# Grouping a pair's transposes in one run of the tensor engine, and spreading value products between keys

## The chip, the cores and the metric

The kernel runs on one core of one Trainium2 chip. The metric is the device time of one execution in microseconds. The engines are PE (matrix products; PEld is its loading of weights), DVE (vector), ACT (scalar), POOL (GpSimd) and SP, which issues the transfers.

## The reference

Windowed attention with 32 global tokens, for 8 batches of 8 heads, and then a feed-forward layer on the result:

```python
s_g = scale * np.matmul(q_g, k_all.transpose(0, 1, 3, 2))
out_g = np.matmul(sm(s_g), v_all)
mask = np.abs(pos[:, None] - pos[None, :]) <= window        # window = 32
s_l = np.concatenate([s_lg, np.where(mask, s_ll, -1e9)], axis=-1)
out_l = np.matmul(sm(s_l), np.concatenate([v_g, v_l], axis=2))
x = np.concatenate([out_g, out_l], axis=2)                   # 8 x 544 tokens x (8 heads x 64)

x_prev = np.concatenate([zeros, x[:, :-1, :]], axis=1)
xk = mu_k * x + (1.0 - mu_k) * x_prev
xr = mu_r * x + (1.0 - mu_r) * x_prev
k = np.maximum(xk @ w_k, 0.0)                                # 512 -> 1024
v = k * k @ w_v                                              # 1024 -> 512
r = 1.0 / (1.0 + np.exp(-(xr @ w_r)))                        # 512 -> 512
out = r * v
```

Local sequences have 512 tokens, global ones 32, heads 64 columns.

## The kernel before

**Number format.** Each feed-forward operand is split into a high and a low part (`h`, `l`), and a product is made of three matmuls (high-high, high-low, low-high). The high part is a cast, the low part the rest: `Keys.part` does both for one half of an operand. The cast is always DVE's (L740), the rest (L741) is DVE's for operands whose name begins with B and POOL's for the others (T1 to T4).

**Two kinds of work.** Attention is done in pairs of units; a unit is two heads of one batch, so a batch has four units in two pairs. The feed-forward layer works on the two token halves of a batch, t0 and t1. While the feed-forward layer of batch b runs, the attention of batch b + 1 is computed, for b = 1 to 6. From batch 2 on, the value product is made for both halves at once by Strassen's scheme: seven products per batch with operands B11, B21, T2 (`values_1`), then T3, T1, T4, B22 (`values_2`). T1 to T4 are differences of the B operands (`Keys.difference`, L733, on DVE). Their left sides lie in DRAM and are loaded as tiles `a`, half a megabyte each, two per product.

**The order is written out by hand.** In this stage PE, ACT, DVE and POOL execute in the order in which the program writes; SP's order is found by a scheduler. `in_turn` goes through a string of letters (`BATCH`): A is the next step of the generator `attention`, F the next step of the batch's feed-forward work (`batch`). One F is 24 matmuls of 128x256. Behind the matmuls of F number n, the entries of the table `todo` for n are written (splits, differences, and `mixing`, which makes xk and xr), and then one entry of the queue `softmaxes` (exponentials of ACT, sums' inverses of DVE, products of POOL for the pair whose scores were last computed).

**A pair's attention before** has seven A steps: four times four transposes of the probabilities (`transposes`, L144; ACT copies each four into `PT`, L414), one step with half of the global transposes, one with the other half and the next pair's scores (128 small matmuls into four banks, reduced on DVE by sixteen instructions, L368), one with the next pair's global scores and this pair's value products (L141 with `PT`).

**Banks of PSUM.** Feed-forward products take the three `ps_m` banks in turn. The transposes take the single `ps_t` bank. The scores take the four `ps_s` banks, and so do, in the same rotation, the global scores (one bank) and the value products (three banks). So the global scores go to the bank in which the first four of the sixteen score blocks lay. A product with `fresh=False` (B22) adds to the bank of an earlier one (T1).

**Feed-forward steps of a batch before** are three products V1, four keys of t0, two gates, four products V2, four keys of t1, two gates.

Of the kernel before, what the change touches and what calls it, by code (L numbers as in the profile page):

```python
# [11 lines left out]
F32R = mybir.dt.float32r  # L12
# [54 lines left out]
def local_global_attention_then_rwkv_ffn(  # L67
# [12 lines left out]
    nc = tc.nc  # L80
# [39 lines left out]
    def psum(tag):  # L120
        if isinstance(use[tag], str):
            tag = use[tag]
        n = turn[tag] = turn.get(tag, -1) + 1
        pool = use[tag][n % len(use[tag])]
        return pool.tile([P, 512], F32, tag="ps", name=f"ps_{tag}")
# [173 lines left out]
        finish(*last)  # L299

    V1 = (("A11", "B11"), ("A12", "B21"), ("S2", "T2"))
    V2 = (("S3", "T3"), ("S1", "T1"), ("A22", "T4"), ("S4", "B22"))
    to_load = [a for a, _ in V1 + V2] * (B - FROM) + ["A11", "A21", "A12", "A22"]
    left = []

# [98 lines left out]
    def pitched(j, h, g0, n):  # L404
        return PT[:, j, h, g0 * PITCH:(g0 + n) * PITCH].rearrange("p (g q) -> p g q", g=n)[:, :, 0:W]

    def transposes(r, h, j=None):

        tp = psum("t")
        for i in range(4):  # L410
            last = transpose(tp[:, i * P:(i + 1) * P], r.Pt[:, 4 * h + i], ident)
        copy = nc.scalar.copy
        if j is not None:
            copy(pitched(j, h, 0, 4), tp.rearrange("p (g q) -> p g q", g=4))  # L414
        else:
            g0 = 2 * r.slots[0][1]
            out = PT[:, :, h, g0 * PITCH:(g0 + 2) * PITCH].rearrange("p j (g q) -> p j g q", g=2)[:, :, :, 0:W]
            copy(out, tp.rearrange("p (j g q) -> p j g q", j=2, g=2))
        return last
# [282 lines left out]
    class Keys:  # L702
# [42 lines left out]
            self.difference(b, i)  # L745
            self.part(b, i)

        def left_over(self, n):

            part, difference = self.part, self.difference  # L750
            todo = (
                ((part, "T2", 1), (difference, "T3", 1)),
                ((part, "T3", 0), (difference, "T4", 0)),
                ((part, "T3", 1), (part, "T1", 0), (difference, "T4", 1)),
                ((part, "T1", 1),),
                ((part, "T4", 0),),
                ((part, "T4", 1), (part, "B22", 0)),
                ((part, "B22", 1),),
            )
            for what, b, i in todo[n]:  # L760
                what(b, i)

        def split(self, *names):
            for b in names:
                self.parts[b] = []
                for val in self.k[b]:
                    tags = Keys.PARTS[Keys.n_parts % len(Keys.PARTS)]
                    Keys.n_parts += 1
                    h, l = (self.tokens[0].two(mlp, f"b{x}", F32R, tag) for x, tag in zip("hl", tags))
                    split(val, h, l, nc.vector if b[0] == "B" else nc.gpsimd)  # L770
                    self.parts[b].append((h, l))

        def product(self, out, b, fresh=True, apart=False, between=None):
            right = self.parts.pop(b)
            steps = [(i, j) for i in range(HC) for j in range(2)]
# [40 lines left out]

        def values_2(self):
            t0, t1 = self.tokens
            u2, u3, c22 = self.u2, self.sum(), self.sum()
            X = self.bank()  # L820
            self.product(X, "T3")
            nc.vector.tensor_add(u3, X, u2)
            yield
            Y = self.bank()
            self.product(Y, "T1")
            nc.vector.tensor_add(c22, Y, u3)
            t1.write(1, c22)
            yield
            X = self.bank()
            self.product(X, "T4")  # L830
            nc.vector.tensor_add(u3, X, u3)
            t0.write(1, u3)
            yield
            self.product(Y, "B22", fresh=False)
            nc.vector.tensor_add(u2, Y, u2)
            t1.write(0, u2)
            yield
# [38 lines left out]
    def attention(pairs):  # L876

        for s in pairs[0]:
            load_qk(s)
        for s in pairs[0]:  # L880
            load_v(s)
        yield
        R = [scores(whole(s)) for s in pairs[0]]
        yield
        Pg = scores_global(pairs[0])
        for pair, nxt in zip(pairs, pairs[1:] + [None]):
            xTs = [xT_of(s.b, s.c) for s in pair]
            for s in nxt or ():
                load_qk(s)
            for j, r in enumerate(R):  # L890
                for h in range(2):
                    transposes(r, h, j)
                    yield
            transposes_global(Pg, (0,))
            yield
            transposes_global(Pg, (1,))
            by_hand = line["all"]
            if nxt:
                R = [scores(whole(s), by_hand) for s in nxt]
                if by_hand:  # L900
                    exps, norm = ([f for r in R for f in of(r)] for of in (lambda r: r.exps, lambda r: r.norm))
                    exps[0]()
                    for i in range(3):
                        softmaxes.append((norm[i], exps[i + 1]))
            yield
            if not by_hand:
                yield
            if nxt:
                Pg, *softmax = scores_global(nxt, later=True)
            copied = weighted(pair, xTs, True)  # L910
            if nxt:
                if by_hand:
                    softmaxes.append((norm[3], softmax[0]))
                    softmaxes.append((softmax[1],))
                else:
                    with tc.issue_after(copied.ins):
                        for f in softmax:
                            f()
            for s in nxt or ():
                load_v(s)  # L920
            yield pair[1].c + 1 == NC
# [146 lines left out]
    def batch(b, before):  # L1068
# [33 lines left out]
        def begin_halves():  # L1102
            nonlocal leftp, sump, gate3
            early_u.close()
            leftp, sump, gate3 = (
                place(name, bufs) for name, bufs in (("leftp", 5), ("sump", 3), ("gate3", 1))
            )
            load_left()
            load_left()
# [22 lines left out]
                15: lambda: (mix_next("r0"), this.difference("T3", 0)),  # L1132
            }
        else:
            steps = chain(before.values_1(), this.keys(t0), gates_of(0), before.values_2(), this.keys(t1), gates_of(1))
            todo = {
                0: lambda: (before.left_over(0), mix(t0, "r2")),
                1: lambda: before.left_over(1),
                2: lambda: before.left_over(2),
                3: lambda: before.left_over(3),  # L1140
                4: lambda: before.left_over(4),
                6: lambda: mix(t1, "k0"),
                7: lambda: mix(t1, "k2"),
                8: lambda: mix(t1, "r0"),
                9: lambda: before.left_over(5),
                10: lambda: (before.left_over(6), mix(t1, "r2")),
                11: lambda: this.part("B11", 0),
                12: lambda: (this.part("B11", 1), this.part("B21", 0)),
                13: lambda: (this.part("B21", 1), this.difference("T1", 0)),
                14: lambda: this.difference("T1", 1),  # L1150
                15: lambda: this.made("T2", 0),
                16: lambda: (this.difference("T2", 1), mix_next("k0")),
                17: lambda: mix_next("k2"),
                18: lambda: (mix_next("r0"), this.difference("T3", 0)),
            }
        for n, _ in enumerate(steps):
# [10 lines left out]
    def keys_at(b):  # L1167
# [2 lines left out]
        return keys_of[b]  # L1170

    BATCH = {
        FROM - 1: "AFAFAFAFAF" "AFFAFFF" "AFAFAFAFAF" "AFFAFFF",
        FROM: "AFAFAFAFAF" "AFAF" "AFAFAFAFAF" "AFFAFF",
        None: "AFAFAFAFAF" "AFFAFF" "AFAFAFAFAF" "AFFFAFF",
    }
    last = first[1]
    change_use(MIDDLE_USE)
# [16 lines left out]
    def end():  # L1195
        change_use(LAST_USE)
        keys, gates = final.keys(t), t.gates()
        values, ends = chain(last.values_1(), last.values_2()), final.values_of_one()
        at, to = last.part, last.difference
        todo = (  # L1200
            lambda: (at("T2", 1), to("T4", 0)),
            lambda: (to("T4", 1), to("T3", 1), at("T3", 0)),
            lambda: (at("T3", 1), at("T1", 0)),
            lambda: (at("T1", 1), at("T4", 0)),
            lambda: t.mixing("r2"),
            lambda: (at("T4", 1), at("B22", 0)),
            lambda: None,
            lambda: at("B22", 1),
            lambda: final.part("B11", 0),
            lambda: (final.part("B11", 1), final.part("B21", 0)),  # L1210
            lambda: final.part("B21", 1),
        )
        for n, x in enumerate("VVKVKVKVKVVEGEGEE"):
            next({"K": keys, "V": values, "E": ends, "G": gates}[x], None)
            if n < len(todo):
                todo[n]()
            yield
# [51 lines left out]
```

## Time and profile before

| | |
|---|---|
| median of three runs | 657.32 us (654.34 to 665.51) |
| profiled execution | 657.44 us |
| its span | 655.7 us |
| busy share of the span: PE, DVE, POOL, ACT | 96%, 78%, 53%, 52% |
| transfers | 127 MB, 194 GB/s |
| clock of PE granted over the span | 0.995 |

In the profile, `L141` is the one line that records all matmuls, and `L144` the one for transposes, so groups are told apart by tile names: `ps_m` feed-forward, `ps_s` scores and value products, `ps_t` transposes. Consecutive matmuls overlap: one has a modelled duration of 0.28 us, but the next starts 0.12 us after it.

The batches lie in the span like this: 1 from 125 to 200 us, 2 to 267, 3 to 340, 4 to 411, 5 to 482, 6 to 550; batch 7, which has no attention beside it, to 604; then the global tokens to the end.

### The profile page before, as it was taken

To read this page: it belongs to the slowest core of one execution; us is meant where nothing else is said; L and a number is where in the kernel's file an instruction comes from. 1 tells how busy PE (TensorE), PEld (TensorE's weight loads), DVE (VectorE), ACT (ScalarE), POOL (GpSimd) and SP (SyncE) were. 2 spreads that over 40 slices of the span, in tenths; PEclk is the share of its full clock that TensorE was granted. 3 is DMA by queue.
4 is the path that set the end of the run, shared out by engine and by line. 5 is a ranking of instruction groups with operands and counts; after the bars stand their busy time and mean duration, and the time that the engine had idled before them with its cause. 6 is when DMAs were issued, how large, how long until landed. Compare 5 with 4: busy or idle time off the path is not lost.

```text
span 655.7 us, 20533 instructions
## 1 busy us (share of the span) xinstructions
PE 630.7 (96%) x8362; PEld 599.6 (91%) x8362; DVE 510.9 (78%) x1308; ACT 338.4 (52%) x1062; POOL 348.4 (53%) x318
## 2 busy tenths in 40 slices
PE   6789899999999989999999999999999999999998
PEld 3567889999989989989999999989999999999997
DVE  4699986556898677986989698986898687787980
ACT  4888686637263576464463727364745533314111
POOL 6377775334856242764357443855366535652840
PEclk9799999999999999999999999999999999999999
DMA  9826534538366922727555584737383562462774
GB/s 333 353 98 241 177 137 163 170 111 307 128 218 208 332 95 73 278 57 289 204 214 190 193 303 163 240 110 267 136 288 103 190 229 67 144 227 79 240 232 170
DMA packets 43565, 127.15 MB, mean 194 GB/s; under 512 B 4048, under 2 KB 20944, under 8 KB 43472
## 3 DMA queue, kind: packets, MB, share of 16 engines
q1 hardware_dynamic: 43472, 125.85, 54.6%
q8 instruction: 66, 1.08, 0.6%
q14 instruction: 27, 0.22, 0.1%
HBM read 108.53 MB, written 17.30 MB: 192 GB/s over the span
## 4 chain that ended last, share of the span: by engine, by line
PE 78%; DVE 10%; DMA 4%; ACT 3%; POOL 2%; issue 2%; SPq 1%; DVEq 0%; ACTq 0%; POOLq 0%
PE ps_m L141 60%; PE ps_s L141 12%; PE ps_t L144 4%; DMA w<-w_k 2%; DMA w<-w_v 1%; DVE diff L614 1%; DVE xfull L582 1%; PE ps_t L141 1%; POOL wv_l L240 1%; ACT Pt L374 1%; DVE a L272 1%; DVE ps_s L230 1%; DVE ps_s L227 1%; DVE kkl L641 1%; DVE bh L740 1%
## 5 line engine op out<-in xcount | busy, mean ns | idle before, releaser
L141 PE MATMUL ps_m<-xkh,wk_h 128*128 128x256 f32 x544 | 155.6, 286 | 2.7 <-DVE gate L685 0.9
L141 PE MATMUL ps_m<-xkl,wk_h 128*128 128x256 f32 x544 | 151.6, 279 | 1.2 <-POOL xkl L587 1.2
L141 PE MATMUL ps_m<-xkh,wk_l 128*128 128x256 f32 x544 | 150.9, 278 | 0.0
L141 PE MATMUL ps_m<-bh,a 128*128 128x256 f32 x736 | 137.3, 283 | 0.0
L380 POOL TENSOR_TENSOR Pt<-Pt,ssum 128x512 f32<-128x512 f32 x64 | 69.6, 1093 | 89.5 <-DVE ssum L333 45.5
L141 PEld LDWEIGHTS ps_m<-bh,a 128*128 128x128 f32 x736 | 115.0, 189 | 0.0
L141 PEld LDWEIGHTS ps_m<-xkh,wk_h 128*128 128x128 f32 x544 | 102.2, 188 | 8.5 <-issue 2.4
L374 ACT ACTIVATE Pt<-Pt,m 128x128 f32<-128x128 f32 x256 | 99.2, 390 | 16.8 <-DVE m L368 16.5
L141 PEld LDWEIGHTS ps_m<-xkl,wk_h 128*128 128x128 f32 x544 | 102.5, 188 | 2.1 <-POOL xkl L587 1.4
L141 PE MATMUL ps_m<-bl,a 128*128 128x256 f32 x368 | 103.0, 280 | 0.0
L141 PEld LDWEIGHTS ps_m<-xkh,wk_l 128*128 128x128 f32 x544 | 102.4, 188 | 0.0
L656 ACT ACTIVATE relu<-ps_m 128x512 f32<-128x512 f32 x52 | 31.0, 596 | 90.3 <-PE ps_m L141 89.8
L141 PE MATMUL ps_m<-xrh,wr_h 128*128 128x256 f32 x272 | 77.0, 283 | 0.0
L141 PE MATMUL ps_m<-xrl,wr_h 128*128 128x256 f32 x272 | 75.6, 278 | 0.0
L141 PE MATMUL ps_m<-xrh,wr_l 128*128 128x256 f32 x272 | 75.4, 278 | 0.0
L619 POOL TENSOR_TENSOR xkl<-xfull,xkh 128x512 fp32r<-128x512 f32 x30 | 39.7, 1325 | 66.5 <-DVE ssum L332 43.1
L141 PEld LDWEIGHTS ps_m<-bl,a 128*128 128x128 f32 x368 | 69.6, 189 | 0.0
L414 ACT COPY PT<-ps_t 128x512 f32<-128x512 f32 x56 | 32.8, 585 | 67.7 <-PE ps_t L144 67.7
L619 POOL TENSOR_TENSOR xrl<-diff,xrh 128x512 fp32r<-128x512 f32 x30 | 40.7, 1356 | 46.8 <-DVE xrh L618 29.8
L368 DVE CUSTOM_DVE_ANT_0 Pt<-ps_s,masks 128x128 f32<-128x128 f32 x256 | 55.9, 285 | 12.0 <-PE ps_s L141 12.0
L141 PE MATMUL ps_s<-raw_qk 64*32 64x128 f32 (+1 forms) x2112 | 55.4, 287 | 5.4 <-DMA raw_qk<-qk 5.4
L741 POOL TENSOR_TENSOR bl<-B,bh 128x512 fp32r<-128x512 f32 x36 | 51.9, 1459 | 14.3 <-DVE bh L740 13.9
(128 smaller groups left out, 1522.1 us busy)
## 6 DMA issues: line engine op xcount, KB each, us to landing
a<-scratch SPq DMA_DIRECT2D x92, 512.0 KB, 4.8
raw_v<-v SPq DMA_DIRECT2D x32, 896.0 KB, 7.6
raw_qk<-qk SPq DMA_DIRECT2D x32, 624.0 KB, 5.5
out_l<-gate SPq DMA_DIRECT2D x32, 256.0 KB, 4.1
w<-w_k SPq DMA_DIRECT2D x8, 512.0 KB, 9.4
w<-w_v SPq DMA_DIRECT2D x8, 512.0 KB, 4.1
w<-w_r SPq DMA_DIRECT2D x4, 512.0 KB, 3.2
scratch<-wv_h SPq DMA_DIRECT2D x8, 256.0 KB, 3.8
```

The costliest lines, as they stand in the source:

```text
L141: return in_line(nc.tensor.matmul(*a, **kw))
L144: return in_line(nc.tensor.transpose(*a, **kw))
L227: nc.vector.tensor_scalar(bits, word(I32, 1), 3, 0x7FFFFFF8, op0=ALU.logical_shift_left, op1=ALU.bitwise_and)
L230: nc.vector.scalar_tensor_tensor(bits, word(I32, 1), -(2 ** 31), bits, op0=ALU.bitwise_and, op1=ALU.bitwise_or)
L240: engine.tensor_sub(lo, val, hi.bitcast(F32))
L368: read = nc.vector.tensor_tensor_reduce(out=Pt[:, i], in0=place(t, n, h), in1=masks[:, 2 * slots[t][1] + n], op0=ALU.add, op1=ALU.min, sca ...
L374: nc.scalar.activation(Pt[:, i], Pt[:, i], AF.Exp, bias=low_x[:, i:i + 1], scale=-1.0, accum_out=ssum[:, i:i + 1],)
L380: nc.gpsimd.tensor_mul(Pt[:, some], Pt[:, some], inv.unsqueeze(2).to_broadcast([P, 4, W]))
L414: copy(pitched(j, h, 0, 4), tp.rearrange("p (g q) -> p g q", g=4))
L619: nc.gpsimd.tensor_sub(lo[:, both], xf, hi[:, both].bitcast(F32))
L656: nc.scalar.activation(rk, kp, AF.Relu)
L741: (nc.vector if b[0] == "B" else nc.gpsimd).tensor_sub(l, val, h.bitcast(F32))
```

## The change

Four things change in the stage that is ordered by hand. First, the sixteen transposes of a pair and the first half of the global ones form one A step, and the sixteen write the four `ps_s` banks instead of taking turns in `ps_t`; a pair has three A steps. Second, the F steps of a batch come in another order: keys stand between the value products. Third, T4's product comes before T1's, and its sum has a tile of its own (`sump` has four). Fourth, `todo` places the splits and differences elsewhere, and `BATCH` the A steps. The number of matmuls, splits and softmax instructions stays.

```diff
@@ V2
-    V2 = (("S3", "T3"), ("S1", "T1"), ("A22", "T4"), ("S4", "B22"))
+    V2 = (("S3", "T3"), ("A22", "T4"), ("S1", "T1"), ("S4", "B22"))
@@ transposes
-    def transposes(r, h, j=None):
+    def transposes(r, h, j=None, bank="t"):
 
-        tp = psum("t")
+        tp = psum(bank)
@@ attention
+            by_hand = line["all"]
             for j, r in enumerate(R):
                 for h in range(2):
-                    transposes(r, h, j)
-                    yield
+                    transposes(r, h, j, "s" if by_hand else "t")
+                    if not by_hand:
+                        yield
             transposes_global(Pg, (0,))
             yield
             transposes_global(Pg, (1,))
-            by_hand = line["all"]
@@ values_2
-            u2, u3, c22 = self.u2, self.sum(), self.sum()
+            u2, u3, c21, c22 = self.u2, self.sum(), self.sum(), self.sum()
             X = self.bank()
             self.product(X, "T3")
             nc.vector.tensor_add(u3, X, u2)
             yield
+            X = self.bank()
+            self.product(X, "T4")
+            nc.vector.tensor_add(c21, X, u3)
+            t0.write(1, c21)
+            yield
             Y = self.bank()
             self.product(Y, "T1")
             nc.vector.tensor_add(c22, Y, u3)
             t1.write(1, c22)
-            yield
-            X = self.bank()
-            self.product(X, "T4")
-            nc.vector.tensor_add(u3, X, u3)
-            t0.write(1, u3)
             yield
             self.product(Y, "B22", fresh=False)
@@ batch, from batch 3 on
-            steps = chain(before.values_1(), this.keys(t0), gates_of(0), before.values_2(), this.keys(t1), gates_of(1))
+            streams = {
+                "V": chain(before.values_1(), before.values_2()), "K": chain(this.keys(t0), this.keys(t1)),
+                "G": chain(gates_of(0), gates_of(1)),
+            }
+            steps = (next(streams[x]) for x in "VVKVKKKGGVKVKVKVKGG")
...
-                9: lambda: before.left_over(5),
-                10: lambda: (before.left_over(6), mix(t1, "r2")),
-                11: lambda: this.part("B11", 0),
-                12: lambda: (this.part("B11", 1), this.part("B21", 0)),
...
+                9: lambda: (at("T4", 1), at("B22", 0)),
+                10: lambda: mix(t1, "r2"),
+                13: lambda: (at("B22", 1), this.part("B11", 0)),
+                14: lambda: (this.part("B11", 1), this.part("B21", 0), this.difference("T1", 0)),
...
     BATCH = {
-        FROM - 1: "AFAFAFAFAF" "AFFAFFF" "AFAFAFAFAF" "AFFAFFF",
-        FROM: "AFAFAFAFAF" "AFAF" "AFAFAFAFAF" "AFFAFF",
-        None: "AFAFAFAFAF" "AFFAFF" "AFAFAFAFAF" "AFFFAFF",
+        FROM - 1: "FAFFAFFAFFFF" "AFFAFFAFFFFFFF",
+        FROM: "AFFAFFAFFF" "AFFAFFAFFFFF",
+        None: "AFFAFFAFFFFF" "AFFAFFAFFFFFF",
     }
@@ end
-        for n, x in enumerate("VVKVKVKVKVVEGEGEE"):
+        for n, x in enumerate("VVKVKVKVVKVEGEGEE"):
```

In the string of 19 steps the products are numbers 0, 1, 3 (B11, B21, T2) and 9, 11, 13, 15 (T3, T4, T1, B22); the table's entries for 15 to 18 and 0 to 3 hold the rest of the splits, differences and mixings.

PE at the start of batch 4, before: the last two matmuls of a gate, the first four transposes, and the first value product, whose operand is `b` and whose left side is `a`.

```order
L141 MATMUL ps_m<-xrl,wr_h 128x256
L141 MATMUL ps_m<-xrh,wr_l 128x256
L144 MATMUL ps_t<-ident,Pt 128x128 x4
L141 MATMUL ps_m<-bh,a 128x256
L141 MATMUL ps_m<-bl,a 128x256
L141 MATMUL ps_m<-bh,a 128x256 x2
```

The same place now:

```order
L141 MATMUL ps_m<-xrl,wr_h 128x256
L141 MATMUL ps_m<-xrh,wr_l 128x256
L144 MATMUL ps_s<-ident,Pt 128x128 x16
L144 MATMUL ps_t<-ident,Pg 96x128 x2
L144 MATMUL ps_t<-ident,Pg 128x128
L141 MATMUL ps_m<-bh,a 128x256
L141 MATMUL ps_m<-bl,a 128x256
```

Three further groups of four transposes and the global one, which stood each behind 24 matmuls, have moved up to the first group.

DVE in the second pair of a batch, before: the evictions of the T4 and B22 products (L831, L835), the splits of B22, B11 and B21 (a cast and the rest each), a difference, and then the first reduction of the pair's scores.

```order
L831 TENSOR_TENSOR sum<-ps_m,sum 128x512
L740 CAST bh<-B_6923 128x512
L741 TENSOR_TENSOR bl<-B_6923,bh 128x512
L835 TENSOR_TENSOR sum<-ps_m,sum 128x512
L740 CAST bh<-B_6923 128x512
L741 TENSOR_TENSOR bl<-B_6923,bh 128x512
L740 CAST bh<-B_6924 128x512
L741 TENSOR_TENSOR bl<-B_6924,bh 128x512
L740 CAST bh<-B_6924 128x512
L741 TENSOR_TENSOR bl<-B_6924,bh 128x512
L733 TENSOR_TENSOR B_6923<-B_7531,B_6923 128x512
L368 ISA Pt,m<-ps_s,masks 128x128
```

Now the splits stand behind the pair's reductions, behind those of its global scores (L442), and behind the eviction of T1's product (L806, number 13):

```order
L442 ISA Pg,mg<-ps_s,nothing,mg 128x480
L442 ISA mg 128x1
L806 TENSOR_TENSOR sum<-ps_m,sum 128x512
L740 CAST bh<-B_5072 128x512
L741 TENSOR_TENSOR bl<-B_5072,bh 128x512
L740 CAST bh<-B_5817 128x512
L741 TENSOR_TENSOR bl<-B_5817,bh 128x512
L332 TENSOR_SCALAR ssum<-ssum 128x4
L333 RECIPROCAL ssum<-ssum 128x4
L740 CAST bh<-B_5817 128x512
L741 TENSOR_TENSOR bl<-B_5817,bh 128x512
L740 CAST bh<-B_5818 128x512
```

All of them come before the first pair's reductions of the next batch, which DVE now reaches like this, from the eviction of the B21 product (L783, number 1 of the next batch) over the differences of T4:

```order
L733 TENSOR_TENSOR B_6245<-B_6247,B_6245 128x512
L614 SCALAR_TENSOR_TENSOR diff<-diff,mu_r_sb,xT 128x256 x2
L618 CAST xrh<-diff 128x512
L783 TENSOR_TENSOR sum<-ps_m,sum 128x512
L740 CAST bh<-B_6244 128x512
L733 TENSOR_TENSOR B_5818<-B_5818,T_6692 128x512 x2
L368 ISA Pt,m<-ps_s,masks 128x128
```

Before, the eviction of the T2 product and four more casts stood ahead of these reductions, which came five F steps into the batch; now they come two F steps into it.

More of the change, by code (lines that the diff above doesn't have):

```diff
@@ L746, in made @@
             self.part(b, i)
[L748 to L771, printed above, removed]
         def product(self, out, b, fresh=True, apart=False, between=None):
@@ L1105, in begin_halves @@
             leftp, sump, gate3 = (
-                place(name, bufs) for name, bufs in (("leftp", 5), ("sump", 3), ("gate3", 1))
+                place(name, bufs) for name, bufs in (("leftp", 5), ("sump", 4), ("gate3", 1))
             )
@@ L1134, in batch @@
         else:
-            steps = chain(before.values_1(), this.keys(t0), gates_of(0), before.values_2(), this.keys(t1), gates_of(1))
-            todo = {
[L1137 to L1141, printed above, removed]
+            streams = {
[3 more added lines that the diff above has]
+            steps = (next(streams[x]) for x in "VVKVKKKGGVKVKVKVKGG")
+            at, to = before.part, before.difference
+            todo = {
+                0: lambda: (at("T2", 1), to("T3", 1), mix(t0, "r2")),
+                1: lambda: (at("T3", 0), to("T4", 0), to("T4", 1)),
+                2: lambda: (at("T3", 1), at("T1", 0)),
+                3: lambda: (at("T1", 1), at("T4", 0)),
                 6: lambda: mix(t1, "k0"),
@@ L1144, in batch @@
                 8: lambda: mix(t1, "r0"),
-                9: lambda: before.left_over(5),
-                10: lambda: (before.left_over(6), mix(t1, "r2")),
-                11: lambda: this.part("B11", 0),
-                12: lambda: (this.part("B11", 1), this.part("B21", 0)),
[L1149 to L1153, printed above, removed]
+                9: lambda: (at("T4", 1), at("B22", 0)),
+                10: lambda: mix(t1, "r2"),
+                13: lambda: (at("B22", 1), this.part("B11", 0)),
+                14: lambda: (this.part("B11", 1), this.part("B21", 0), this.difference("T1", 0)),
+                15: lambda: (this.difference("T1", 1), this.part("B21", 1)),
+                16: lambda: (this.made("T2", 0), mix_next("k0")),
+                17: lambda: (this.difference("T2", 1), mix_next("k2")),
                 18: lambda: (mix_next("r0"), this.difference("T3", 0)),
@@ L1200, in end @@
         todo = (
-            lambda: (at("T2", 1), to("T4", 0)),
-            lambda: (to("T4", 1), to("T3", 1), at("T3", 0)),
+            lambda: (at("T2", 1), to("T3", 1)),
+            lambda: (at("T3", 0), to("T4", 0), to("T4", 1)),
             lambda: (at("T3", 1), at("T1", 0)),
@@ L1207, in end @@
             lambda: None,
-            lambda: at("B22", 1),
-            lambda: final.part("B11", 0),
+            lambda: None,
+            lambda: (at("B22", 1), final.part("B11", 0)),
             lambda: (final.part("B11", 1), final.part("B21", 0)),
```

## The prediction

> **What bounds the kernel now.** I read the page first, then the busy time by stretches, then the chain of waits inside one batch, then PE's own waits.
>
> ```profile
> span 655.7 us, 20533 instructions
> PE 630.7 (96%) x8362; PEld 599.6 (91%) x8362; DVE 510.9 (78%) x1308; ACT 338.4 (52%) x1062; POOL 348.4 (53%) x318
> ```
>
> The profiled execution took 657.44 us: the span and 1.7 us around it. The median of the three runs is 657.32 us, so the sum below, made on 657.44, needs no correction. PE is busy for 96% of the span, so what the change can win is idle time of PE or time that PE spends on switching; what it can lose is any wait that reaches PE. By stretches (busy us of PE, PEld, DVE, ACT, POOL, then the granted clock), one batch with waits and one without:
>
> ```profile
> 200.30:266.80 66.50, 63.72 (x926) 60.72 (x926) 50.60 (x151) 37.39 (x122) 27.82 (x25) 1.00 0.52 189
> 339.70:410.70 71.00, 71.00 (x998) 68.66 (x997) 59.99 (x159) 38.38 (x125) 38.70 (x31) 1.00 0.59 209
> ```
>
> Batch 2 (200 to 267) leaves PE idle for 2.8 us; batch 4 (340 to 411) none at all. In batch 4 DVE is busy for 60 of 71 us, so it is the next limit, with 11 us to spare. The chain of waits in the batch that starts at 410.7 (start, length, what) is all PE:
>
> ```profile
> 410.89 0.44 PE ps_t L144 x4
> 411.33 2.83 PE ps_m L141 x24
> ...
> 414.60 2.74 PE ps_m L141 x24
> ...
> 423.79 0.33 PE ps_t L144 x3
> ...
> 427.18 1.98 PE ps_s L141 x127
> ```
>
> This gives PE's prices: four transposes 0.44, three of the global scores 0.33, one feed-forward step of 24 matmuls (an F turn) 2.83 or 2.74 (I take 2.78), scores 1.98.
>
> **Part 1, fewer switches.** PE's timeline, first matmul after a run of eight transposes:
>
> ```profile
> 70.42 1.03 PE L144 MATMUL ps_t<-ident,Pt 128*128 128x128 f32 x8
> 71.21 0.36 PE L141 MATMUL ps_m<-xrh,wr_h 128*128 128x256 f32 x1
> 71.41 0.28 PE L141 MATMUL ps_m<-xrl,wr_h 128*128 128x256 f32 x1
> ```
>
> From 70.42 to 71.41, less one matmul's 0.12, eight transposes cost 0.87; four cost 0.44. The part that doesn't grow with the count is 2 x 0.44 - 0.87 = 0.01 us per run. The change turns seven attention turns per pair into three, in 12 pairs: 48 x 0.01 = **-0.5 us**. A switch is nearly free here. The transposes now use the four ps_s banks; the next writer is the scores, two F turns (5.6 us) later, and ACT's four copies fit into that.
>
> **Part 2, PE's old waits.** PE's waits after 125 us (total, times, longest):
>
> ```profile
> PE ps_t L144 <- POOL Pt L380: 1.3, 1, 1.3
> PE ps_t L144 <- POOL Pg L453: 1.0, 1, 1.0
> PE ps_t L144 <- ACT PT L484: 0.9, 1, 0.9
> ```
>
> All three are transposes, in batch 2 and early in batch 3, which stood too close behind the softmax that feeds them. Idle time is counted from a matmul's modelled end, 0.28 after its start, while the next would start after 0.12: each is worth 0.16 more, so 3.2 + 0.5 = 3.7. Afterwards batch 2 has three F turns (8.3 us) between the value products and the next run of transposes, and five in its second half; the second global part comes two F turns behind the first. I count **-3.7 us**, at worst 0.
>
> **Part 3, DVE's queue.** DVE executes in the order written. Before, the parts of B22, B11 and B21 were split while PE did the value products between transposes, ahead of the pair's scores reductions. Now they are split after them: from the eviction of the T1 product (turn 13) DVE has one unbroken queue that reaches over the batch's end to the sixteen reductions of the next pair's scores. DVE's prices from its timeline, start to start:
>
> ```profile
> 383.50 0.87 DVE L614 SCALAR_TENSOR_TENSOR diff<-diff,mu_r_sb,xT 128x256 f32<-128x256 f32 x2
> 384.40 0.43 DVE L618 CAST xrh<-diff 128x512 fp32r<-128x512 f32 x1
> 384.75 0.68 DVE L831 TENSOR_TENSOR sum<-ps_m,sum 128x512 f32<-128x512 f32 x1
> 385.35 1.14 DVE L740 CAST bh<-B 128x512 fp32r<-128x512 f32 x1
> ...
> 388.73 0.41 DVE L740 CAST bh<-B 128x512 fp32r<-128x512 f32 x1
> 389.17 1.68 DVE L741 TENSOR_TENSOR bl<-B,bh 128x512 fp32r<-128x512 f32 x1
> 390.78 0.41 DVE L740 CAST bh<-B 128x512 fp32r<-128x512 f32 x1
> 391.23 0.69 DVE L741 TENSOR_TENSOR bl<-B,bh 128x512 fp32r<-128x512 f32 x1
> 391.84 0.42 DVE L740 CAST bh<-B 128x512 fp32r<-128x512 f32 x1
> ...
> 396.88 0.69 DVE L733 TENSOR_TENSOR B<-B,B 128x512 f32<-128x512 f32 x1
> 397.48 0.16 DVE L332 TENSOR_SCALAR ssum<-ssum 128x4 f32<-128x4 f32 x1
> ...
> 403.44 0.75 DVE L609 TENSOR_TENSOR diff<-xT 128x256 f32<-128x256 f32 x2
> ...
> 405.42 0.16 DVE L332 TENSOR_SCALAR ssum<-ssum 128x4 f32<-128x4 f32 x1
> ```
>
> ```profile
> 428.30 0.29 DVE L368 CUSTOM_DVE_ANT_0 Pt<-ps_s,masks 128x128 f32<-128x128 f32 x1 [1.36 <-PE ps_s L141]
> ...
> 431.69 0.17 DVE L332 TENSOR_SCALAR ssum<-ssum 128x4 f32<-128x4 f32 x1
> ...
> 431.98 1.57 DVE L609 TENSOR_TENSOR diff<-xT 128x256 f32<-128x256 f32 x2
> ```
>
> Free prices: an r mixing 1.25, an eviction 0.60, a split on DVE (cast and rest) 1.06, a difference 0.60, a k mixing 1.98, sixteen reductions 3.39, an inverse of the sums 0.29; a cast alone 0.45. The queue holds 5 splits (5.3), 2 k and 2 r mixings (3.96 and 2.5), 8 differences (4.8), 3 casts (1.35), 3 evictions (1.8) and 3 inverses (0.87): 20.6 us. But the second split above shows that these prices don't always hold: 389.17 takes 1.68 instead of 0.69, because POOL works on another tensor in that time:
>
> ```profile
> 388.88 1.43 POOL L699 TENSOR_TENSOR gate<-sum,gate 128x512 f32<-128x512 f32 x1 [1.23 <-DVE sum L835]
> ```
>
> How much that stretches a full queue, two stretches show in which DVE never waited:
>
> ```profile
> 377.30:393.50 16.20, 16.20 (x253) 15.82 (x251) 15.87 (x23) 4.00 (x8) 7.67 (x6) 1.00 0.89 305
> 409.90:426.90 17.00, 17.00 (x150) 17.00 (x149) 16.83 (x21) 6.15 (x12) 14.32 (x11) 1.00 0.68 229
> ```
>
> In the first, DVE did 6 splits, a cast, 4 evictions, an r mixing, a difference and an inverse: 11.4 at free prices, in 16.1 us, a factor of 1.42 with 6 POOL instructions (0.37 per us). In the second: 2 r mixings, 4 differences, 6 casts, 2 evictions and an inverse, 9.1 in 17.0, a factor of 1.87 with 11 (0.65 per us). The new queue has 13 POOL instructions beside it, some 0.42 per us, near the first stretch; I take 1.5: 20.6 x 1.5 = 30.9 us.
>
> What PE gives it: from the end of turn 13 there are five F turns to the batch's end (13.9), 19 transposes (2.1), two F turns (5.6), global transposes and scores (2.3), two F turns (5.6): 29.5 us until the global scores and value products, whose first bank is free when four reductions are done (0.85). 30.9 + 0.85 - 29.5 = 2.3 us of wait. Behind the reductions DVE still has the evictions of T2 and the inverses, and ACT's exponentials wait for them; those have two to five F turns, so they aren't late. A nearer wait lies inside: turn 17 needs the bank that DVE empties after turn 15, behind (3.0 + 3.0) x 1.5 + 0.6 = 9.6 us of queue where PE gives 8.3; but what PE loses there it doesn't lose again at the scores. The queue of this length stands ahead of batches 4, 5 and 6 (batch 2's steps end lighter): 3 x 2.3 = **+7 us**. Its ends: at 1.42 the wait is 0.6 (sum 2); at 1.7, halfway to the dense stretch, 6.4 (sum 19); below zero it can't be, since these reductions made nobody wait before.
>
> The trace agrees with a rule of the Trainium skill (page GPSIMD Engine Reference, section 8, Key points): GpSimd shares its SBUF interfaces with VectorE, and DVE instructions with two SBUF inputs, or in a two-port mode, contend with it. Taken as full exclusion, that rule is a rival below.
>
> **Part 4, the rest.** Value products between keys leave each product's loads more F turns; PE's waits above name none of these loads, and SP's next pair of query loads is still issued behind the global scores, a whole half batch ahead: 0. Part and sum tiles (sump with four) cost no instruction: 0. The pace of matmuls is not constant:
>
> ```profile
> 544.81 107.63 PE ps_m L141 x912
> ```
>
> These 912 run at 0.118 each, the 2.83 pace; at the 2.74 pace (0.114) they would take 3.5 us less. Which pace follows a switch the trace doesn't explain; I leave it as it is, with -3.5 to +3 for the range.
>
> **Sum.** 657.4 - 0.5 - 3.7 + 7 = 660.2, so **660 us**.
>
> **Rivals.** (a) *No new wait*: POOL's work falls where DVE evicts from PSUM and the factor stays under 1.38, so the queue ends in time: 657.4 - 4.2 = 653. For it: 11 us of spare DVE time per batch; against it: none of that spare lies in this queue. (b) *DVE becomes the bound, slower than before*: if every POOL instruction holds DVE for its whole time, 1.3 us (14.32 / 11), 13 of them add 16.9 to the 20.6, the queue takes 37.5 and each of the three batches waits 8.9: 657.4 - 4.2 + 26.7 = 680; it passes 2% once the factor is about 1.7. Against full exclusion: in the dense stretch 14.3 us of POOL and 9.1 of free DVE work fit into 17.0. Taken alone and at its strictest, the rule of the Trainium skill's page GPSIMD Engine Reference would make it this. (c) *Pace*: no new wait, and the matmuls fall into the 2.74 pace: 653 - 3.5 - 3 = 646.5. (d) *The change doesn't do what it says*: batch 2's softmax still ends behind its three F turns and the old waits return as one: 660.2 + 3.7 = 664.
>
> **Chances.** Forecast 0.40, (a) 0.27, (b) 0.13, (c) 0.08, (d) 0.12. The range 648 to 671 holds the forecast with its factor between 1.42 and 1.7, (a) and (d), and leaves out most of (b) and part of (c). About 2% is what a measurement can tell from no change. Faster by over 2% (under 644.3) needs (c) and more: 0.05; slower (over 670.5) is (b): 0.11; the rest 0.84.
>
> **What would show it.** Right: PE's waits name no transposes on POOL Pt or Pg in batch 2; in batches 4 to 6 a wait of some 2 us at the global scores or value products on DVE's reductions (L368), or at a feed-forward matmul on DVE's eviction; DVE without a gap from turn 13 to the reductions. Wrong: PE idle elsewhere, reductions that start with the scores, or a DVE gap in that queue.

## The result and the profile after

The changed kernel takes 675.9 us (median of 6 runs) where the kernel before takes 657.8: a ratio of 1.027, 95% interval 1.021 to 1.033, so it is slower. The profiled execution took 677.24 us, 19.8 more than that of before. First the page of the changed kernel (span, busy time, and the granted clock of TensorE in 40 slices, 9 being 90% or more):

```profile
span 675.5 us, 20516 instructions
PE 638.1 (94%) x8362; PEld 604.5 (89%) x8362; DVE 515.3 (76%) x1308; ACT 336.6 (50%) x1062; POOL 351.9 (52%) x318
PEclk9899999999999999999998999899997999999999
```

The work is the same, 8362 matmuls. What is new is in the third line: a clock of 0.8 and 0.7 in three places late in the kernel, where the kernel before has 9 in every slice but one at the start. The busy time by batches (us of PE, PEld, DVE, ACT, POOL, then clock), with the last row of the kernel before behind those of the changed one:

```profile
200.40:263.00 62.60, 62.60 (x927) 60.13 (x926) 45.61 (x149) 37.44 (x124) 24.99 (x23) 1.00 0.48 172
337.40:414.50 77.10, 73.25 (x999) 70.56 (x998) 61.39 (x159) 38.19 (x125) 38.85 (x31) 0.98 0.56 191
414.50:492.60 78.10, 74.28 (x999) 71.13 (x998) 61.93 (x159) 38.20 (x125) 38.90 (x31) 0.96 0.55 189
492.60:563.00 70.40, 66.89 (x822) 64.84 (x821) 49.72 (x108) 29.98 (x89) 33.26 (x25) 0.95 0.45 142
616.00:675.50 59.50, 54.31 (x457) 53.50 (x455) 40.00 (x53) 11.18 (x17) 23.68 (x17) 1.00 0.58 186
```

```profile
604.20:655.70 51.50, 48.22 (x410) 48.02 (x408) 33.43 (x42) 9.44 (x14) 20.43 (x15) 1.00 0.63 205
```

Batch 2 lost its 2.8 us of idle PE, as the prediction said. Batches 4 to 6 now leave PE idle for 3.5 to 3.9 us each, and the clock fell to 0.98, 0.96 and 0.95 there. Batch 4 is 77.1 us long instead of 71.0. The last stretch leaves PE idle for 5.2 us instead of 3.3. PE's waits after 125 us (total, times, longest), without one of 0.2 us:

```profile
PE ps_s L141 <- DVE m L368: 10.7, 4, 3.5
PE ps_m L141 <- issue: 1.5, 1, 1.5
PE ps_t L144 <- POOL Pg L453: 1.5, 3, 0.9
PE ps_m L141 <- DVE sum L810: 1.1, 3, 0.4
PE ps_m L141 <- POOL bl L741: 1.1, 1, 1.1
PE ps_m L141 <- DVE bh L740: 0.8, 1, 0.8
```

The first row is the wait that the prediction named, at the global scores behind DVE's reductions: three times 3.5 idle, 3.6 counted from the matmuls' starts (the fourth, in batch 3, is 0.2). The last two are one place, in the last stretch: a product waits for the split of its operand. The chain of waits over the end of batch 4 shows the first in full:

```profile
429.55 3.35 DVE B L733 x2
432.90 0.20 DVE Pt L368
...
433.89 7.13 PE ps_s L141 x116
```

DVE works off the differences of T4 (L733), starts the reductions at 432.9, and PE's global scores follow at 433.89. Those scores and the value products, 116 matmuls, then take 7.13 us; before, the same 116 took 4.27 (row further below). The granted clock in stretches of 3.41 us around that place:

```profile
429.32:432.73 3.41, 1.08 (x12) 0.82 (x10) 3.41 (x3) 0.00 (x0) 3.03 (x2) 1.00 0.37 95
432.73:436.15 3.42, 2.26 (x14) 1.22 (x16) 3.42 (x32) 2.85 (x11) 0.00 (x0) 0.50 0.82 286
436.15:439.56 3.41, 3.41 (x68) 3.41 (x66) 3.38 (x9) 3.11 (x18) 2.80 (x3) 0.50 0.82 272
439.56:442.97 3.41, 3.41 (x61) 3.29 (x60) 2.88 (x7) 1.68 (x8) 3.41 (x3) 1.00 1.04 392
```

PE was busy for 1.08 of 3.41 us, and for the next 6.8 us its clock was 0.50. The prediction had no such term. Summed over the eight stretches from batch 1 on, PE's idle time rose from 8.4 to 20.2 us, by 11.8; the half clock lasted 3.41, 6.83 and 6.83 us in batches 4, 5 and 6, and half of that is 8.5. Together 20.3, against 19.8 measured.

### The profile page after: what moved, and what is told of

It is laid out like the page before. It is cut to its first block, busy times and chain, and to the rows that moved or that the text cites. A ratio compares the mean times of both kernels' runs of the same rounds, so it can differ in the third digit from the quotient of the medians.

```text
span 675.5 us, 20516 instructions
## 1 busy us (share of the span) xinstructions
PE 638.1 (94%) x8362; PEld 604.5 (89%) x8362; DVE 515.3 (76%) x1308; ACT 336.6 (50%) x1062; POOL 351.9 (52%) x318
## 3 DMA queue, kind: packets, MB, share of 16 engines
q8 instruction: 66, 1.08, 0.6%
## 4 chain that ended last, share of the span: by engine, by line
PE 64%; DVE 23%; DMA 4%; issue 3%; ACT 3%; POOL 2%; SPq 1%; DVEq 0%; POOLq 0%; ACTq 0%
PE ps_m L141 46%; PE ps_s L141 12%; DVE bh L740 4%; DVE B L733 4%; DVE bl L741 3%; PE ps_s L144 2%; DMA w<-w_k 2%; DVE diff L614 2%; PE ps_t L144 2%; DVE diff L609 1%; DMA w<-w_v 1%; ACT Pt L374 1%; DVE xfull L582 1%; POOL wv_l L240 1%; DVE xfull L614 1%
## 5 line engine op out<-in xcount | busy, mean ns | idle before, releaser
L141 PE MATMUL ps_m<-xkh,wk_h 128*128 128x256 f32 x544 | 153.8, 283 | 2.0 <-ACT gate L671 0.9
L141 PE MATMUL ps_m<-bh,a 128*128 128x256 f32 x736 | 135.6, 281 | 0.8 <-DVE bh L740 0.8
L380 POOL TENSOR_TENSOR Pt<-Pt,ssum 128x512 f32<-128x512 f32 x64 | 67.8, 1070 | 71.7 <-DVE ssum L333 36.3
L141 PE MATMUL ps_s<-raw_qk 64*32 64x128 f32 (+1 forms) x2112 | 57.1, 289 | 16.2 <-DVE m L368 10.7
L619 POOL TENSOR_TENSOR xkl<-xfull,xkh 128x512 fp32r<-128x512 f32 x30 | 43.1, 1435 | 53.4 <-DVE xkh L618 35.6
L699 POOL TENSOR_TENSOR gate<-sum,gate 128x512 f32<-128x512 f32 x24 | 35.2, 1466 | 61.3 <-DVE sum L806 28.7
L141 PEld LDWEIGHTS ps_s<-PT,raw_v 128*64 128x64 f32 x1568 | 55.8, 150 | 8.8 <-issue 6.2
```

What stands on the lines that cost most here:

```text
L141: return in_line(nc.tensor.matmul(*a, **kw))
L380: nc.gpsimd.tensor_mul(Pt[:, some], Pt[:, some], inv.unsqueeze(2).to_broadcast([P, 4, W]))
L619: nc.gpsimd.tensor_sub(lo[:, both], xf, hi[:, both].bitcast(F32))
L699: (nc.vector if v.tensor.name.startswith("ps_") else nc.gpsimd).tensor_mul(o, v, o)
```

## The experiments

The theory from this profile: DVE's queue of the prediction makes three waits of 3.6 us, and each wait halves the clock. Rivals: the value products are slow for another reason; one of the two parts of the change costs the time by itself; something other than GpSimd stretches the queue. Each job ran the kernel before on its own chip as well (medians of 663.0 beside the first four experiments, 659.8 beside the others), so kernels of different jobs are compared by their ratios to it.

### The queue made shorter

```diff
-  0: (at("T2", 1), to("T3", 1), mix(t0, "r2")),
-  1: (at("T3", 0), to("T4", 0), to("T4", 1)),
-  2: (at("T3", 1), at("T1", 0)),
-  3: (at("T1", 1), at("T4", 0)),
+  0: (at("T2", 1), mix(t0, "r2")),
+  2: (to("T3", 1), at("T3", 0), to("T4", 0), to("T4", 1)),
+  3: (at("T3", 1), at("T1", 0)),
+  4: (at("T1", 1), at("T4", 0)),
```

> The changed kernel, with four vector instructions groups (the rest of T3's difference, the first split of T3, both differences of T4) written behind the reductions of the scores instead of ahead of them; nothing else changed. In the changed kernel these take 5.1 us of the queue that the reductions stand behind (422.87 to 423.48 and 428.41 to 432.82), more than the 3.6 us that TensorE waits for them. Theory, queue and clock: the three waits of 3.6 us at the global scores go, and with them the half clock behind each and the slow value products (5.2 to 5.6 us, back to 3.6): 3 x (3.6 + 2.5) = 18 less than the changed kernel, about 658. Rival, the value products are slow for another reason (loads or copies beside them): only 3 x 3.6 = 11 less, about 666, and they stay above 5 us.

Ratio to the kernel before 1.002 (0.997 to 1.007), median 662.3; profiled 656.4 (span 654.5), 20.9 less than the changed kernel's profile. DVE's timeline at the first reduction, and the chain of waits behind it:

```profile
419.34 0.28 DVE L368 CUSTOM_DVE_ANT_0 Pt<-ps_s,masks 128x128 f32<-128x128 f32 x1
```

```profile
421.95 4.27 PE ps_s L141 x116
```

The reductions now start 2.6 us ahead of the global scores, and the 116 matmuls take 4.27 again. The whole loss hangs on these four groups of DVE work in front of the reductions. That the value products recover shows only that their slowness came with the wait, not why; the next experiment does.

### The wait kept, but filled

```diff
+  if by_hand and pair[0].c == 0 and pair[0].b >= 5:
+      spare = psum("t")
+      for _ in range(34):
+          transpose(spare[:, 3 * P:], ident, ident)
   Pg, *softmax = scores_global(nxt, later=True)
```

> The changed kernel, with 34 transposes of the identity into the empty ps_t bank ahead of the three global scores that wait (first pair of the batches 4 to 6); they take 34 x 0.11 = 3.7 us, as long as the wait, so TensorE isn't idle there but does nothing useful. Theory, queue and clock: the scores come no earlier, but the granted clock stays at 1.00, scores and value products go back to about 1.0 and 3.6 us: 3 x 2.5 = 7 less than the changed kernel, about 669. Rival, slow for another reason than idleness: value products stay at 5.2 to 5.6 us and the time at 676.

Ratio 1.021 (1.010 to 1.031); span 667.9, 7.6 less than the changed kernel's. PE's timeline at the same place as above, and the clock there:

```profile
428.35 3.87 PE L144 MATMUL ps_t<-ident 128*128 128x128 f32 x34
...
432.44 0.98 PE L141 MATMUL ps_s<-raw_qk 128*64 128x480 f32 x4
433.25 3.63 PE L141 MATMUL ps_s<-PT,raw_v 128*64 128x96 f32 x112
```

```profile
431.00:435.00 4.00, 3.94 (x78) 3.19 (x77) 4.00 (x35) 3.69 (x15) 0.22 (x1) 1.00 0.77 265
```

The useful work starts no earlier relative to the feed-forward step in front, but the clock stays at 1.00 and the value products take 3.63 us. Idleness it was, and it cost 7.6 us beside the waits themselves. The filled kernel has a half clock of its own in its last stretch (637.43 to 640.84, worth 1.7 us) that the changed kernel lacks, so 7.6 is rather too little; the 8.5 counted above fit that. (In the medians, across chips, the gain is 0.6%, with intervals that overlap; the size rests on the profiles.)

### Each part of the change alone

The first kernel is the kernel before with the runs of sixteen transposes and the three switches per pair (the change's edits of `transposes`, of `attention` and of the table of turns); the second is the changed kernel with those edits taken back, so that only the order of products and splits is new.

```diff
 # grouping alone: edits to the kernel before
 ...
-  None: "AFAFAFAFAF" "AFFAFF" "AFAFAFAFAF" "AFFFAFF",
+  None: "AFFAFFAFFFFF" "AFFAFFAFFFFFF",
 ...
```

> The kernel before with one part of the change: all sixteen transposes in one run in the ps_s banks and three switches to attention per pair, with the feed-forward steps and the splits in their old order. Theory, queue and clock: from the eviction of the product in turn 13 on the queue ahead of the reductions has three splits fewer, 3 x 1.06 x 1.5 = 4.8 us, more than the 3.6 us of the wait; no wait at the global scores, and the old waits of batch 2 (3.7 us) go: about 654. Rival, the grouping alone brings the reductions too early: the wait stays at some 3 us and the time is 665 to 676.

> The changed kernel with the seven attention turns of before: the value products between keys and the splits in their new order alone. Theory, queue and clock: the reductions come seven feed-forward steps into the batch instead of four, 8.3 us later for the same queue, so no wait at the global scores; the wait of turn 17 for its bank and the late split at the end stay, 2 to 4 us: about 659. Rival, the new order costs the time by itself (queue so full that the wait shows up elsewhere, for instance at the feed-forward steps): 668 to 676.

Grouping alone: ratio 0.988 (0.978 to 0.997), span 647.2, faster than before, by less than 2%. Order alone: 1.034 (1.023 to 1.045), as slow as the whole change or slower. My expectation for the second was wrong by some 3%; its "seven instead of four" steps are those of the global scores, the reductions come five instead of two steps into the batch. PE's waits after 125 us, all of the grouping alone and then the largest of the order alone (its others are 1.3 us or less):

```profile
PE ps_t L144 <- POOL Pg L453: 1.4, 3, 0.9
PE ps_m L141 <- POOL bl L741: 0.4, 1, 0.4
```

```profile
PE ps_t L144 <- ACT PT L414: 14.5, 4, 5.2
```

With the old turns the new order meets the same queue at another engine. DVE's and ACT's timelines of the order alone:

```profile
361.46 3.45 DVE L733 TENSOR_TENSOR B<-B,T 128x512 f32<-128x512 f32 x2
```

```profile
365.03 0.63 ACT L658 ACTIVATE B<-relu 128x512 f32<-128x512 f32 x1 [6.55 <-DVE B L733]
365.56 0.57 ACT L414 COPY PT<-ps_t 128x512 f32<-128x512 f32 x1
```

ACT stands for 6.55 us at the square of the first keys, whose tile takes the place of one that T4's differences still read; behind it stands the copy of the transposes, and PE's next transposes wait for their bank. Behind each of the three long waits the clock is at 0.50 for 6.8 us. I had looked for this queue only at the reductions. Its profile also fell on an execution with more half clock in its start than the others (0.81 between 20 and 100 us), which makes the profiled 690 longer than its median of 683.7.

What the grouping alone gains beside the old waits is seen in two batches without any wait: the same 116 matmuls one batch apart, before and with the grouping.

```profile
329.94 4.27 PE ps_s L141 x116
...
400.97 4.27 PE ps_s L141 x116
```

```profile
351.62 4.27 PE ps_s L141 x116
...
422.05 4.27 PE ps_s L141 x116
...
579.67 64.35 PE ps_m L141 x564
```

71.03 us against 70.43: 0.60 for eight switches, 0.075 each. The two kernels of the section on a version better than both, which have the grouping too, show 70.43 at the same place. The last row is matmuls of the grouping alone at the end, without attention: 564 in 64.35 us, 0.114 each, where the kernel before had 0.118. But the grouping with one step moved in batch 1, whose last stretch is written the same, needs longer for the same 564:

```profile
582.60 66.68 PE ps_m L141 x564
```

That is 0.118 again, so the pace at the end doesn't come from the grouping; what sets it is open, and some 2 us of the span of 647.2 are owed to it. An estimate of the grouping's own gain from these rows is 48 x 0.075 = 3.6 us of switches and 3.7 us of old waits, less 1.8 us of new ones: 5.5 us. The ratio says 8, with an interval of 2 to 15.

### A wait as short as the predicted one

```diff
 # against the kernel of the filled wait
-      for _ in range(34):
+      for _ in range(13):
```

> The changed kernel with 13 instead of 34 transposes of the identity ahead of the three global scores that wait: 1.4 us of the 3.7 us are filled, 2.3 us stay idle, which is the wait that the prediction gave. In the records so far the granted clock changes in steps of 3.41 us; it was halved behind each wait of 3.7 us and of 4.5 to 5.5 us, and not behind single ones of 1.1 to 2.4 us after 50 us. Theory, a clock that needs a window of that length mostly idle: the clock stays at 1.00 behind the three waits and the value products take 3.6 us; about 670. Rival, any idle time of TensorE above some 2 us halves the clock: value products at 5.2 to 5.6 us, about 677.

669.2 us in one run. Both expectations were too simple: the clock was halved behind one of the three waits, all 2.1 us from the start of one score matmul to that of the next, and not behind the others. The stretches of 3.41 us, laid on the moments at which the clock changed:

```profile
354.06:357.48 3.42, 1.50 (x15) 0.82 (x12) 3.42 (x15) 1.09 (x6) 1.48 (x1) 1.00 0.64 168
357.48:360.89 3.41, 3.41 (x52) 2.89 (x50) 3.41 (x23) 3.32 (x15) 0.95 (x1) 0.50 0.92 323
429.20:432.57 3.37, 2.83 (x27) 2.46 (x25) 3.37 (x3) 0.00 (x0) 3.30 (x3) 1.00 0.34 89
432.57:435.98 3.41, 2.03 (x40) 1.37 (x40) 3.41 (x30) 2.53 (x10) 0.00 (x0) 1.00 0.84 285
504.25:507.66 3.41, 2.52 (x24) 2.14 (x22) 3.41 (x3) 0.00 (x0) 3.00 (x2) 1.00 0.33 89
507.66:511.07 3.41, 2.37 (x52) 1.71 (x52) 3.41 (x32) 2.87 (x11) 0.00 (x0) 1.00 0.85 287
```

The first wait lies inside one stretch and, with two gaps of 0.4 and 0.7 us behind it, leaves PE busy for 1.50 us: half clock follows. The other two fall across a boundary, 2.0 to 2.8 us of each stretch stay busy, and the clock holds. In this one run, then, what a wait of 2 us costs is a matter of where it falls.

### GpSimd's low parts left out

```diff
 ...
   nc.vector.tensor_copy(hi[:, both], xf)
-  nc.gpsimd.tensor_sub(lo[:, both], xf, hi[:, both].bitcast(F32))
+  if lo is not zero:
+      nc.gpsimd.tensor_sub(lo[:, both], xf, hi[:, both].bitcast(F32))
```

> The changed kernel without GpSimd's subtractions that make the low parts of the mixings (L619): TensorE reads a tile of zeros in their place, so that part of the products is left out; every instruction of the other engines stays. Beside the queue of 32.4 us ahead of the reductions that takes away 4 of 13 GpSimd instructions, 5.9 of 18.3 us. Theory, GpSimd stretches the queue (11.8 us over its free price of 20.6, or 0.65 per us of GpSimd): 0.65 x 5.9 = 3.8 us off the queue, the wait of 3.6 us nearly goes and the clock holds: 657 to 661. Rival, something else stretches it (loads, TensorE's or ScalarE's reads): the queue stays at 32 us, the wait at 3.6 us and the time at 675.

Ratio 1.006 (1.002 to 1.009), median 662.5, a little above the expected time. The queue first, from T1's eviction on, in the changed kernel (then two rows of GpSimd's beside it, and the busy times of the whole queue), and the same instructions with the low parts left out, whose lines are numbered two or three higher:

```profile
400.44 0.69 DVE L806 TENSOR_TENSOR sum<-ps_m,sum 128x512 f32<-128x512 f32 x1 [5.63 <-PE ps_m L141]
...
401.50 1.69 DVE L741 TENSOR_TENSOR bl<-B,bh 128x512 fp32r<-128x512 f32 x1
...
417.50 1.85 DVE L609 TENSOR_TENSOR diff<-xT 128x256 f32<-128x256 f32 x2
...
432.82 0.28 DVE L368 CUSTOM_DVE_ANT_0 Pt<-ps_s,masks 128x128 f32<-128x128 f32 x1
```

```profile
401.21 1.43 POOL L699 TENSOR_TENSOR gate<-sum,gate 128x512 f32<-128x512 f32 x1 [6.88 <-DVE sum L806]
...
417.13 1.60 POOL L619 TENSOR_TENSOR xkl<-xfull,xkh 128x512 fp32r<-128x512 f32 x1 [1.75 <-DVE xkh L618]
```

```profile
400.44:432.82 32.38, 29.63 (x370) 28.78 (x368) 31.80 (x46) 9.34 (x19) 18.25 (x13) 1.00 0.56 197
```

```profile
400.69 0.69 DVE L809 TENSOR_TENSOR sum<-ps_m,sum 128x512 f32<-128x512 f32 x1 [5.63 <-PE ps_m L141]
...
417.69 0.75 DVE L611 TENSOR_TENSOR diff<-xT 128x256 f32<-128x256 f32 x2
...
L370 DVE CUSTOM_DVE_ANT_0 Pt<-ps_s,masks x5: 279/281/282, 429.0 to 429.9; 128x128 f32<-128x128 f32 x5
```

From eviction to first reduction 28.3 us instead of 32.4: 4.1 less for 5.9 us of GpSimd less, close to the 3.8 expected, and the wait at the scores is gone. The pair of differences shows it at one spot: 1.85 us beside GpSimd's subtraction, 0.75 without. So GpSimd stretches DVE's queue.

How it does, the two timelines show instruction by instruction. GpSimd's first one runs until 402.64; DVE's subtraction that starts beside it ends at 403.19, 0.55 later, and takes 1.69 instead of its free 0.69. The pair of 417.50 ends at 419.35, 0.6 behind GpSimd's 418.73. It is the same for all 13 GpSimd instructions of this queue and of the two other queues that lead to a wait: each holds up one DVE instruction, a subtraction, a mixing or a cast that reads SBUF, which then ends 0.28 us (casts and the instructions of 256 columns) or 0.55 us (subtractions of 512) behind it. These 13 DVE instructions take 12.0 us more than at free prices, which is the whole stretch of 11.8 us, 0.9 us for each GpSimd instruction. The two evictions from PSUM beside which a GpSimd instruction starts (L810, L783) keep their 0.66 and 0.68 us.

The time came out a little above the range, and two things show beside the theory. In this kernel's profile the clock is at 0.87 between 20 and 100 us, where the changed kernel has 0.98. And the pace is slower: a chain row of this kernel and one of the kernel with the shorter queue, each five feed-forward steps without a wait,

```profile
435.56 14.44 PE ps_m L141 x120
```

```profile
426.22 13.82 PE ps_m L141 x120
```

show matmuls of 0.120 against 0.115. Why those that read the tile of zeros run slower was not tried.

### A version better than both

The grouping alone, with the second half of batch 1 one step later, and the new order repaired:

```diff
 # grouping alone, one step later (against the grouping alone)
-  FROM - 1: "FAFFAFFAFFFF" "AFFAFFAFFFFFFF",
+  FROM - 1: "FAFFAFFAFFFFF" "AFFAFFAFFFFFF",
 # new order repaired (against the changed kernel): the shorter queue, T4's splits ahead of T1's, and
 ...
-  13: (at("B22", 1), this.part("B11", 0)),
 ...
+  11: at("B22", 1),
+  12: this.part("B11", 0),
 ...
```

> The kernel with the grouping only (old order of feed-forward steps and splits), and the second half of batch 1 begun one feed-forward step later, so that the sixteen transposes of its second pair stand further behind the softmax that feeds them (a wait of 1.2 us on GpSimd's Pg). About 1 us less than the grouping alone, so 650 beside a kernel before of 660: a ratio of 0.985, and an interval below 1.00. Rival, the gain of the grouping alone was chance of one chip: a ratio of 0.995 to 1.005.

> The changed kernel with the new order of the value products kept and the splits in the order of the products (T4 ahead of T1, so that B22 and B11 can be split two turns earlier), the four groups behind the reductions as in the first experiment, and the same at the end. Theory: the waits at the scores, most of that at turn 17 (0.6 each) and those at the end (1.1 and 1.5 us and the half clock behind them) go: 654.5 - 1.5 - 3 = 650 for the span, equal to the grouping alone within 0.5%: the new order by itself brings nothing once it doesn't wait. Rival, the new order is worth something of its own: more than 1% below the grouping alone, under 645.

Grouping, later: 0.988 (0.984 to 0.992). Repaired order: 0.992 (0.987 to 0.996), and of PE's waits after 125 us only the three of the transposes on GpSimd's Pg are left, 1.4 us. Both intervals lie below 1.00: both kernels are faster than the kernel before, by about 1%, and than the changed one. The gain of the grouping is not chance of one chip; the extra step brings nothing that shows beside 0.988 of the first grouping, and its profile still has 2.4 us of short waits. The new order, freed of its waits, adds nothing that shows to the grouping.

## Why the prediction was wrong

The forecast was 660 in a range of 648 to 671; the change takes 676. Its mechanism was found in the place and the batches that it named; two prices and some omissions put it off.

**Part 3, the queue: right mechanism, undersized.** The 13 GpSimd instructions are those counted, and what PE gave was 29.6 us (400.44 to the first of the global scores, at 430.07) against 29.5. The queue took 32.4 us instead of 30.9: a factor of 1.57 on the free price, not 1.5. The factor stands for 13 DVE instructions that each waited for a GpSimd instruction, 12.0 us in all. A difference of 5% in the queue made the wait 3.6 us instead of 2.3, and the three together 10.7 instead of 7. A wait is the difference of two numbers of some 30 us, and the text gave its factor as if 1.5 were better known than the two stretches, 1.42 and 1.87, allow.

**Part 3, what the wait costs: the step that failed.** "3 x 2.3" takes a wait to cost its own length. It put the clock behind the waits at nothing, without a reason. Behind each of them the clock was at 0.50 for 3.4 to 6.8 us, some 8.5 us in all; filled with useless transposes, the same waits cost 7.6 us less. Without those 8.5 us the changed kernel's profile would stand at 668.7, inside the range; the filled one's stood at 669.65. The Trainium skill (page TensorE: Matmul & The Clock Gate, Part 1 and "Why this matters for your kernels") describes a free-running window of 3413 ns and warns of idle gaps above some 3 us. The trace agrees with the window: all changes in the changed kernel after 100 us lie whole multiples of 3.41 us apart. That warning belonged to the upper end of the wait in Part 3; it was left out.

**Part 1, switches: too small.** The price of 0.01 us counted the gap at the transposes alone. Two batches without waits give 0.075 per switch, so 48 of them would be 3.6 us instead of 0.5. Most of it is pace: 120 matmuls in one run take 13.82 us (the row of the shorter queue), 2.76 for 24, where the steps between switches took 2.83 and 2.74 in turn; over the 19 steps of the two batches the feed-forward rows add up to 53.1 us before and 52.6 grouped, 0.5 of the 0.6. The prediction had both rows and put them under pace, as if switches had no part in it.

**Part 2, old waits: right, but not all of it.** Batch 2's waits are gone. New ones on GpSimd's Pg came in batches 1 and 3, 1.5 us in all, because only batch 2 was looked at.

**Part 3, the nearer wait.** The wait of turn 17 for its bank is there: 0.4 us each, 1.1 in all, where the text's own numbers, 9.6 against 8.3, gave 1.3 each. What PE lost there it didn't lose again at the scores, as the text said: the 29.6 us hold it.

**Part 4.** No load kept PE waiting after 125 us, as it said. The end was not costed: T4's product stands two steps behind T3's there, and the split that it needs is written between them, behind a mixing that took 3.0 us beside GpSimd's four subtractions, and 1.9 us of waits follow; with T4's splits ahead of T1's they are gone.

**Rivals.** (b) gave nearly this time, 680, by luck: it charged GpSimd's whole time to the queue, 16.9 us, which would have made each wait 8.9 us and left the clock alone. The queue shows 11.8 us of stretch for 18.3 us of GpSimd, 0.65 per us (0.69 by the low parts left out). Its mechanism was nearer than its size: one DVE instruction did stand still for each GpSimd instruction, but only from the moment when DVE came to it, with what it had begun and the evictions from PSUM done beside GpSimd. The Trainium skill (page GPSIMD Engine Reference, section 8, Key points) names this contention, of DVE instructions in a two-port mode or with two SBUF inputs. The trace agrees: subtractions, mixings and casts were held up, evictions were not. The point from which it passes 2% was put at a factor of 1.7; with the clock's share it was passed at 1.57. (a) and (d) didn't occur. (c), the faster pace up to the end, showed in the profile of the grouping alone (0.114), but not in those of the two better kernels that share it (0.118). What would show it right was all seen, except for the length of the wait; what was missing from that list is the clock behind it.

Not settled: the wait of 1.5 us put down to "issue" (at 285 us), for which no releaser shows, in the changed kernel and, as long or longer, in those with filled waits. In all three traces a packet of 16 KB of the instruction queue begins within half a microsecond of it (284.46 us, the wait from 284.93 in the changed kernel); in the shorter queue it comes at 281.25 and there is no wait. That is a lead, not a cause that was shown. Open, too, is what sets the pace of the matmuls, 0.114 or 0.118.

## What to carry to other kernels

When work is moved on a helper engine, write down its queue from the last common point to each instruction that the busy engine needs, for every engine that stands in between, and compare it with what the busy engine gives. Count GpSimd's instructions beside a DVE queue that reads SBUF: here each held one DVE instruction up, 0.9 us on average. Here, too, moving four groups behind one consumer undid the whole loss. Price a wait of the matmul engine that comes near 2 us with the granted clock behind it, not with its length alone. Try the parts of a change apart: here one part was worth 1.2%, and the other cost as much as both together.

## What the runs showed of the hardware

The clock follows a fixed grid of 3.41 us. In the ten profiles, with the idle time in each stretch of that grid after 100 us added up from the matmuls' starts, every stretch at full clock with up to 2.0 us idle was followed by full clock, and every one with some 2.4 us or more by half clock, for one or two stretches; waits of 1.1 and 1.5 us close together count as one. In the kernel with the shorter queue those two, at its end, did it:

```profile
619.66:623.07 3.41, 1.46 (x11) 1.07 (x10) 3.38 (x4) 0.47 (x1) 2.58 (x2) 1.00 0.49 137
623.07:626.48 3.41, 3.41 (x19) 3.41 (x18) 0.83 (x2) 0.00 (x0) 0.51 (x1) 0.50 0.19 43
```

The Trainium skill (page TensorE: Matmul & The Clock Gate, "Why this matters for your kernels") sets the bound at a gap of some 3 us between matmuls. That is too lenient for these runs: a wait of 2.1 us with smaller gaps behind it in one stretch was enough once, and halved the clock for 3.4 us.

GpSimd held DVE up instruction by instruction: in the three queues ahead of the waits each of the 39 GpSimd instructions delayed one DVE instruction that reads SBUF, which ended 0.28 or 0.55 us behind it.
